# Pinned TensorE order in the second layer, one block transpose placed later, the second product one tile further behind

## The chip, the cores and the metric

The kernel runs on one core of a Trainium2 chip. The metric is device time in microseconds of one execution; the time before is the median of three runs. The engines are TensorE (PE, its weight loads shown apart as PEld), VectorE (DVE), ScalarE (ACT), GpSimd (POOL) and SyncE (SP), which issues nearly all DMAs here.

## What is computed

Three stages follow each other: attention within chunks of 64 tokens, a first feed-forward layer with g = h·cos(h), and a second feed-forward layer whose activation is h·softmax(h), normalised over its 1024 columns. All is in float32. The change touches the second layer alone.

```python
def _moe2_ref(x, w_in, w_out, g_ln):          # x 4608x512, w_in 512x1024, w_out 1024x512
    h = x @ w_in
    h_max = np.max(h, axis=-1, keepdims=True)
    e = np.exp(h - h_max)
    sm = e / (np.sum(e, axis=-1, keepdims=True) + 1e-09)
    solu = h * sm
    mu = np.mean(solu, axis=-1, keepdims=True)
    var = np.mean((solu - mu) ** 2, axis=-1, keepdims=True)
    ln = (solu - mu) / np.sqrt(var + 1e-06) * g_ln
    return (ln @ w_out).astype(np.float32)
```

## The kernel before

**Precision.** Every float32 operand of a product is split into a high and a low part, and a product is three matmuls: high·high, high·low, low·high, each 128x128 weights against 512 columns.

**The second layer, first product.** The 4608 tokens are 36 tiles of 128, taken two at a time: 18 pairs, i = 0 to 17. The product x·w_in of a pair is made from seven block products (a Strassen-like scheme), spread over four segments: `pair(i, seg)` issues 12, 12, 6 and 12 matmuls for seg 0, 1, 2, 3, that is 42 for a pair, on the lines L862 to L864 in `prod`. The results land in PSUM tiles h2 that rotate over three buffers, so a segment takes over the buffer of the segment three before it: (i, 3) that of (i, 0). ACT (L902) and DVE (L887, L890) add the blocks up in SBUF; L902 and the first L890 free the buffer of (i, 0). Of the four SBUF tiles that the pairs' results rotate over, the one of the second tile of an odd pair is taken from the pool tag "w".

**Between the products.** `stats(i, e)` and `norm(i, e)` (e = 0, 1 for the two tiles of the pair) make softmax and normalisation one pair later, on ACT, DVE and POOL. `blocks32(i, e)` transposes the result in 32x32 blocks on DVE into a tile bt that holds four tiles, group j (L964). When the four tiles of group j are there, after pair 2j+1, `shuffle(j)` issues 16 DMAs on SP (L974) that carry the blocks to four tiles lt, which are the transposed tiles t = 4j to 4j+3. `split_ln(t)` makes the high and low parts lh (ACT) and ll (DVE), both on L104.

**Second product.** `mm_o(t, half)` issues 12 matmuls of ln·w_out (L992, L993, L994: lh·whi, lh·wlo, ll·whi), half 0 for the first 512 of the 1024 rows, half 1 for the others; `store(t)` copies the sum (ACT, L998, tile os) and issues four DMAs on SP. Tiles lt, lh, ll and the odd pairs' result share the pool tag "w" of 32 slots with the weights of the layer (22 of them).

**The order.** Segments are counted x = 4i + seg. The last loop goes over x: it traces the segment (i, seg), then at even x the split of the next tile and the store of the one before, and then 12 matmuls of tile t = 2i − 7 + seg//2. So in the source's order TensorE alternates 12 (or 6) matmuls of h with 12 of o, and the first tile of group j, t = 4j, comes at the place (2j+3, 2), three segments after its shuffle was traced at (2j+2, 3). Segments up to (3, 0) are traced in the loop of the first layer, beside its last steps.

**Who orders.** The framework plans the order of each engine's instructions itself, by its own account of when operands and buffers are there, and by the source's order among those that are ready. An instruction issued through an `InOrder` wrapper while its flag is set is pinned behind all that was traced before it on its engine. In the second layer no instruction is pinned before the change. Each engine then works through its own list in that order.

Of the kernel before, what the change touches and what calls it, by code (L numbers as in the profile page):

```python
# [29 lines left out]
def kernel(  # L30
# [12 lines left out]
    nc = tc.nc  # L43
# [8 lines left out]
    SUB = T // P  # L52
    NI = NT // P
    KD = DM // P
    NF = F1 // P
    NF2 = F2 // P
# [52 lines left out]
            return call  # L109

    pe, act, dve = InOrder(nc.tensor), InOrder(nc.scalar), InOrder(nc.vector)
    sync = InOrder(nc.sync, in_order_loads)

    def split(src, hi, lo, mul=None):

        if mul is None:
            act.activation(out=hi, in_=src, func=AF.Copy)
            dve.tensor_tensor(out=lo, in0=src, in1=hi.bitcast(F32), op=ALU.subtract)
        else:
            nc.scalar.activation(out=hi, in_=src, func=AF.Copy, scale=mul)  # L120
            nc.vector.scalar_tensor_tensor(
                out=lo, in0=src, scalar=mul, in1=hi.bitcast(F32), op0=ALU.mult, op1=ALU.subtract
            )
# [32 lines left out]
    def wtile(dt, name, n=1024):  # L156
        return wp.tile([P, n], dt, tag="w", name=name)
# [528 lines left out]
    def load_y(i):  # L686
        t = sp_.tile([P, 7 * 256], F32, tag="st", name="yr")
        nc.sync.dma_start(out=t, in_=y_dram[i // 2][i % 2])
        yr[i] = t
# [19 lines left out]
    if True:  # L709
# [23 lines left out]
        for c in range(4):  # L733
            sync.dma_start(
                out=gcol[32 * c:32 * (c + 1)],
# [103 lines left out]
        for i in range(SUB, NU):  # L839
            j, o = divmod(UNITS[i][0] * CH, T)  # L840
# [17 lines left out]
        def prod(i, ps, operand, key):  # L858
            for kk in range(2):
                a, b = (y[i][operand][:, kk * P:(kk + 1) * P] for y in (yh, yl))  # L860
                whi, wlo = w2in[key, kk]
                nc.tensor.matmul(out=ps, lhsT=a, rhs=whi, start=kk == 0, stop=False)  # L862
                nc.tensor.matmul(out=ps, lhsT=a, rhs=wlo, start=False, stop=False)  # L863
                nc.tensor.matmul(out=ps, lhsT=b, rhs=whi, start=False, stop=kk == 1)  # L864

        def h2tile(i, e):
            x = (2 * i + e) % 4
# [51 lines left out]
        def stats(i, e):  # L919
            h2 = hA.pop((i, e))  # L920
            nm = ap_.tile([P, 1], F32, tag="nm", name="nm", bufs=4)
            ss = ap_.tile([P, 1], F32, tag="ss", name="ss", bufs=4)
            nc.vector.tensor_scalar(out=nm, in0=tops.pop((i, e, 1)), scalar1=-1.0, scalar2=None, op0=ALU.mult)
            ex = ap_.tile([P, 1024], F32, tag="t", name="e", bufs=2)
            nc.scalar.activation(out=ex, in_=h2, func=AF.Exp, bias=nm, accum_out=ss)
            nc.vector.tensor_scalar(out=ss, in0=ss, scalar1=1e-9, scalar2=None, op0=ALU.add)
            nc.vector.reciprocal(out=ss, in_=ss)
            mu = ap_.tile([P, 1], F32, tag="mu", name="mu", bufs=4)
            nc.vector.scalar_tensor_tensor(
                out=h2, in0=h2, scalar=ss, in1=ex, op0=ALU.mult, op1=ALU.mult, accum_out=mu  # L930
            )
            nc.vector.tensor_scalar(out=mu, in0=mu, scalar1=-1.0 / F2, scalar2=None, op0=ALU.mult)
            va = ap_.tile([P, 1], F32, tag="va", name="va", bufs=4)
            nc.scalar.activation(out=ex, in_=h2, func=AF.Square, bias=mu, accum_out=va)
            nc.vector.tensor_scalar(
                out=va, in0=va, scalar1=1.0 / F2, scalar2=1e-6, op0=ALU.mult, op1=ALU.add
            )
            rs = ap_.tile([P, 1], F32, tag="rs", name="rs", bufs=4)
            nc.gpsimd.tensor_tensor(out=rs, in0=va, in1=nhalf, op=ALU.pow)
            nc.gpsimd.tensor_tensor(out=mu, in0=mu, in1=rs, op=ALU.mult)  # L940
            solu[i, e], nmu[i, e], rstd[i, e] = h2, mu, rs

        def norm(i, e):
            so = solu[i, e]
            nc.scalar.activation(
                out=so, in_=so, func=AF.Identity, scale=rstd.pop((i, e)), bias=nmu.pop((i, e))
            )
# [6 lines left out]
        def blocks32(i, e):  # L954
            j, n = i // 2, i % 2 + 2 * e
            if j not in blks:
                if j == 0:
                    blks[j] = [wtile(F32, "bt").rearrange("p (q n t) -> p q n t", q=8, n=SUB) for _ in range(4)]
                else:
                    t = sp[0].tile([P, 32, SUB, 32], F32, tag="bt", name="bt", bufs=1)  # L960
                    blks[j] = [t[:, 8 * c:8 * (c + 1)] for c in range(4)] + [t]
            src = solu.pop((i, e)).rearrange("p (b f) -> p b f", f=32)
            if j:
                nc.vector.transpose(out=blks[j][4][:, :, n], in_=src)  # L964
            else:
                for c in range(4):
                    nc.vector.transpose(out=blks[j][c][:, :, n], in_=src[:, 8 * c:8 * (c + 1)])

        def shuffle(j):
            b = blks.pop(j)  # L970
            for a in range(4):
                l = wtile(F32, "lt")
                for c in range(4):
                    nc.sync.dma_start(  # L974
                        out=l[32 * c:32 * (c + 1)],
                        in_=b[c][32 * a:32 * (a + 1)].rearrange("p q n t -> p (q n t)"),
                    )
                lnp[j, a] = l

        def split_ln(j, a):  # L980
            hi, lo = wtile(F32R, "lh"), wtile(F32R, "ll")
            split(lnp.pop((j, a)), hi[:], lo[:])
            lnh[j, a], lnl[j, a] = (x.rearrange("p (f c) -> p f c", c=P) for x in (hi, lo))

        def mm_o(j, a, half):
            if half == 0:
                ops[j, a] = ps_h.tile([P, DM], F32, tag="h", name="o")
            o = ops[j, a]
            for f in range(half * NF2 // 2, (half + 1) * NF2 // 2):
                hi, lo = lnh[j, a][:, f], lnl[j, a][:, f]  # L990
                whi, wlo = w2out[f]
                nc.tensor.matmul(out=o, lhsT=hi, rhs=whi, start=(f == 0), stop=False)  # L992
                nc.tensor.matmul(out=o, lhsT=hi, rhs=wlo, start=False, stop=False)  # L993
                nc.tensor.matmul(out=o, lhsT=lo, rhs=whi, start=False, stop=(f == NF2 - 1))  # L994

        def store(j, a):
            s = sp[0].tile([P, DM], F32, tag="os", name="os")
            nc.scalar.activation(out=s, in_=ops.pop((j, a)), func=AF.Copy)  # L998
            for n in range(SUB):
                t0 = j * T + n * P + 32 * a  # L1000
                queue = nc.scalar if n % 2 and (j, a) == (NJ - 1, SUB - 1) else nc.sync
                queue.dma_start(out=out[t0:t0 + 32, :], in_=s[32 * n:32 * (n + 1)])

        def segment(i, seg):

            if i < NPAIR:
                pair(i, seg)
            if 0 <= i - 1 < NPAIR:
                e = seg // 2
                if seg % 2 == 0:  # L1010
                    stats(i - 1, e)
                else:
                    norm(i - 1, e)
                    blocks32(i - 1, e)
                    if e and (i - 1) % 2:
                        shuffle((i - 1) // 2)
            if i + 1 < NPAIR:
                if seg == 1:
                    load_y(i + 1)
                elif seg == 3:  # L1020
                    split_y(i + 1)
# [4 lines left out]
        for n in range(NSTEP + LAG + 1):  # L1026
# [50 lines left out]
            if rest >= 6:  # L1077
                segment((rest - 6) // 4, (rest - 6) % 4)
# [1 line left out]
        sp.append(ctx.enter_context(tc.tile_pool(name="sp", bufs=2, reuse_waits="tile")))  # L1080


        LAG2 = 7
        first_seg = 4 * EARLY + 1
        split_ln(0, 0)
        for x in range(first_seg, 2 * (NI + LAG2) + 4):
            i, seg = divmod(x, 4)
            segment(i, seg)
            t, half = 2 * i - LAG2 + seg // 2, seg % 2
            if half == 0:  # L1090
                if 0 <= t + 1 < NI:
                    split_ln(*divmod(t + 1, SUB))
                if 0 <= t - 1 < NI:
                    store(*divmod(t - 1, SUB))
            if 0 <= t < NI:
                mm_o(*divmod(t, SUB), half)


# [25 lines left out]
```

## Time and profile before

| what | us |
|---|---|
| median of three runs | 1317.0 (1316.44 to 1317.3) |
| the profiled execution | 1315.48 |
| its span, first to last instruction | 1313.7 |
| TensorE busy | 1270.9, 97% of the span |
| VectorE busy | 977.1, 74% |
| ScalarE busy | 789.3, 60% |

The span begins with attention, then runs the first layer to about 948 us and the second layer from 867 us on, the two overlapping; from 964 us on only the second layer is left. The granted clock of TensorE was 0.992 in the mean. A matmul's row shows its start and a duration of 0.39 us; since matmuls are pipelined, the step from one start to the next is what counts.

### The profile page before, as it was taken

How to read it: one execution, taken by the hardware profiler on the slowest of the kernel's cores; microseconds unless marked ns; L12 is line 12 of the kernel's file. 1: busy time of each engine (PE TensorE's matmuls, PEld its weight loads, DVE VectorE, ACT ScalarE, POOL GpSimd, SP SyncE). 2: the span in 40 equal slices, each digit the busy share in tenths (PEclk: the TensorE clock that was granted, in tenths of full speed). 3: DMA queues.
4: the chain of work that ended last, by engine and by line, in shares of the span. 5: the costliest groups of instructions: out<-in, count | busy, mean ns of one | idle time of the engine just before them, and what ended most of it. 6: DMA issues, size and time to landing. Idle time of an engine off the chain costs nothing.

```text
span 1313.7 us, 20245 instructions
## 1 busy us (share of the span) xinstructions
PE 1270.9 (97%) x7652; PEld 1016.4 (77%) x7652; DVE 977.1 (74%) x1608; ACT 789.3 (60%) x1143; POOL 30.7 (2%) x79
## 2 busy tenths in 40 slices
PE   5899999999999999999999999999989999999998
PEld 4566777888887787888887888888768888888886
DVE  4887988676779879878878866667786686766751
ACT  4877876666655656556556545537665655655552
POOL 0000000000000000000000000000110000000000
PEclk9899999999999999999999999999989999999999
DMA  9942344331344344353343410450464543445224
GB/s 243 212 108 82 111 132 92 90 77 30 58 135 135 63 133 133 65 124 97 78 108 97 95 27 1 150 215 28 154 190 114 149 131 99 122 111 145 64 63 107
DMA packets 240930, 143.44 MB, mean 109 GB/s; under 512 B 176832, under 2 KB 217280, under 8 KB 239296
## 3 DMA queue, kind: packets, MB, share of 16 engines
q1 hardware_dynamic: 240736, 142.02, 41.4%
q8 instruction: 60, 0.98, 0.3%
q14 instruction: 38, 0.31, 0.1%
q10 hardware_dynamic: 96, 0.13, 0.0%
HBM read 83.63 MB, written 39.58 MB: 94 GB/s over the span
## 4 chain that ended last, share of the span: by engine, by line
PE 76%; DVE 10%; ACT 5%; issue 4%; SPq 3%; DMA 2%; POOL 0%; ACTq 0%; DVEq 0%; POOLq 0%
PE h L570 8%; PE y L637 8%; PE y L638 7%; PE y L639 7%; PE h L572 7%; PE h L571 7%; PE o L994 5%; PE o L992 5%; PE o L993 5%; PE h L862 4%; PE h L864 3%; PE h L863 3%; SPq L104 3%; DVE z L104 2%; PE x L104 1%
## 5 line engine op out<-in xcount | busy, mean ns | idle before, releaser
L570 PE MATMUL h<-xh,whi 128*128 128x512 f32 x576 | 232.6, 404 | 1.6 <-ACT xh L104 1.3
L571 PE MATMUL h<-xl,whi 128*128 128x512 f32 x576 | 226.2, 393 | 0.9 <-DVE xl L104 0.9
L572 PE MATMUL h<-xh,wlo 128*128 128x512 f32 x576 | 226.2, 393 | 0.1
L637 PE MATMUL y<-gh,whi 128*128 128x512 f32 x544 | 213.0, 397 | 4.8 <-ACT gh L104 3.8
L638 PE MATMUL y<-gl,whi 128*128 128x512 f32 x544 | 215.3, 396 | 0.3 <-DVE gl L104 0.3
L639 PE MATMUL y<-gh,wlo 128*128 128x512 f32 x544 | 214.9, 395 | 0.0
L599 ACT ACTIVATE r<-r 128x512 f32<-128x512 f32 x144 | 90.8, 631 | 166.0 <-DVE r L593 165.7
L607 DVE SCALAR_TENSOR_TENSOR hs<-r,hs 128x512 f32<-128x512 f32 x136 | 93.7, 689 | 81.6 <-ACT r L600 81.2
L570 PEld LDWEIGHTS h<-xh,whi 128*128 128x128 f32 x576 | 108.8, 189 | 27.9 <-issue 1.6
L104 ACT ACTIVATE gh<-hs 128x512 fp32r<-128x512 f32 x136 | 85.5, 629 | 74.0 <-DVE hs L607 71.0
L571 PEld LDWEIGHTS h<-xl,whi 128*128 128x128 f32 x576 | 108.7, 189 | 25.0 <-issue 1.7
L572 PEld LDWEIGHTS h<-xh,wlo 128*128 128x128 f32 x576 | 108.6, 189 | 24.2 <-issue 0.5
L104 DVE TENSOR_TENSOR gl<-hs,gh 128x512 fp32r<-128x512 f32 x136 | 93.4, 687 | 44.8 <-ACT gh L104 44.6
L637 PEld LDWEIGHTS y<-gh,whi 128*128 128x128 f32 x544 | 101.4, 188 | 31.7 <-ACT gh L104 7.5
L638 PEld LDWEIGHTS y<-gl,whi 128*128 128x128 f32 x544 | 102.2, 188 | 26.2 <-DVE gl L104 2.3
L639 PEld LDWEIGHTS y<-gh,wlo 128*128 128x128 f32 x544 | 102.1, 188 | 23.6
L577 ACT ACTIVATE hs<-h 128x512 f32<-128x512 f32 x144 | 85.2, 592 | 56.7 <-PE h L572 46.2
L992 PE MATMUL o<-whi,lh 128*128 128x512 f32 x288 | 113.5, 394 | 1.6 <-ACT lh L104 1.6
L994 PE MATMUL o<-whi,ll 128*128 128x512 f32 x288 | 113.2, 393 | 0.7 <-DVE ll L104 0.5
L993 PE MATMUL o<-wlo,lh 128*128 128x512 f32 x288 | 113.3, 393 | 0.0
L590 DVE SCALAR_TENSOR_TENSOR r<-kt,hs 128x512 f32<-128x512 int32 x144 | 99.1, 688 | 16.4 <-ACT kt L585 13.9
L862 PE MATMUL h<-whi,yh 128*128 128x512 f32 x252 | 99.6, 395 | 9.9 <-DVE tp L890 9.9
(112 smaller groups left out, 2078.3 us busy)
## 6 DMA issues: line engine op xcount, KB each, us to landing
lt<-bt SPq DMA_DIRECT2D x144, 128.0 KB
yr<-yd SPq DMA_DIRECT2D x18, 896.0 KB
yd<-ts SPq DMA_DIRECT2D x18, 512.0 KB
out<-os SPq DMA_DIRECT2D x142, 64.0 KB
vi<-in_v SPq DMA_DIRECT2D x64, 128.0 KB
qi<-in_q SPq DMA_DIRECT2D x224, 32.0 KB
ki<-in_k SPq DMA_DIRECT2D x224, 32.0 KB
st<-in_moe_w_in SPq DMA_DIRECT2D x10, 512.0 KB
```

Source lines behind the costliest of these rows:

```text
L104: ins = getattr(self.engine, name)(*args, **kwargs)
L570: nc.tensor.matmul(out=t, lhsT=wa, rhs=xh[j][:, kk, :], start=(kk == 0), stop=False)
L571: nc.tensor.matmul(out=t, lhsT=wa, rhs=xl[j][:, kk, :], start=False, stop=False)
L572: nc.tensor.matmul(out=t, lhsT=wb, rhs=xh[j][:, kk, :], start=False, stop=(kk == KD - 1))
L590: nc.vector.scalar_tensor_tensor(out=r, in0=kt, scalar=-TWO_PI_HI, in1=h, op0=ALU.mult, op1=ALU.add)
L637: nc.tensor.matmul(out=o, lhsT=wa, rhs=a, start=head, stop=False)
L638: nc.tensor.matmul(out=o, lhsT=wa, rhs=b, start=False, stop=False)
L639: nc.tensor.matmul(out=o, lhsT=wb, rhs=a, start=False, stop=last)
L862: nc.tensor.matmul(out=ps, lhsT=a, rhs=whi, start=kk == 0, stop=False)
L992: nc.tensor.matmul(out=o, lhsT=hi, rhs=whi, start=(f == 0), stop=False)
L993: nc.tensor.matmul(out=o, lhsT=hi, rhs=wlo, start=False, stop=False)
L994: nc.tensor.matmul(out=o, lhsT=lo, rhs=whi, start=False, stop=(f == NF2 - 1))
```

## The change

There are four edits.

1. A second wrapper `pe2` of TensorE with a flag of its own, `late`, off at first. The matmuls of `prod` and of `mm_o` go through it. The flag is set just before the last loop, so from the segment (3, 1) on each matmul of both products is pinned behind everything that was traced before it on TensorE.
2. In `segment`, the block transposes of the pair's first tile, `blocks32(i−1, 0)`, are traced in seg 2, ahead of the statistics of the second tile, and no longer in seg 1. Those of the second tile stay in seg 3.
3. The tile of the second product is read from a list `order` with one entry for each half pair: seven empty places, tiles 0 to 13, one empty place, tiles 14 to 35, one empty place. So tiles 0 to 13 stand where they stood, the segments (10, 2) and (10, 3) have no matmul of the second product, and from tile 14 on each tile comes one half pair (two segments) later than before.
4. Split and store follow the list: the split of the next entry and the store of the entry before.

The number of instructions and their shapes are the same.

```diff
--- before.py
+++ after.py
@@ -109,6 +109,9 @@
             return call
 
     pe, act, dve = InOrder(nc.tensor), InOrder(nc.scalar), InOrder(nc.vector)
+
+    late = [False]
+    pe2 = InOrder(nc.tensor, late)
     sync = InOrder(nc.sync, in_order_loads)
 
     def split(src, hi, lo, mul=None):
@@ -859,9 +862,9 @@
             for kk in range(2):
                 a, b = (y[i][operand][:, kk * P:(kk + 1) * P] for y in (yh, yl))
                 whi, wlo = w2in[key, kk]
-                nc.tensor.matmul(out=ps, lhsT=a, rhs=whi, start=kk == 0, stop=False)
-                nc.tensor.matmul(out=ps, lhsT=a, rhs=wlo, start=False, stop=False)
-                nc.tensor.matmul(out=ps, lhsT=b, rhs=whi, start=False, stop=kk == 1)
+                pe2.matmul(out=ps, lhsT=a, rhs=whi, start=kk == 0, stop=False)
+                pe2.matmul(out=ps, lhsT=a, rhs=wlo, start=False, stop=False)
+                pe2.matmul(out=ps, lhsT=b, rhs=whi, start=False, stop=kk == 1)
 
         def h2tile(i, e):
             x = (2 * i + e) % 4
@@ -989,9 +992,9 @@
             for f in range(half * NF2 // 2, (half + 1) * NF2 // 2):
                 hi, lo = lnh[j, a][:, f], lnl[j, a][:, f]
                 whi, wlo = w2out[f]
-                nc.tensor.matmul(out=o, lhsT=hi, rhs=whi, start=(f == 0), stop=False)
-                nc.tensor.matmul(out=o, lhsT=hi, rhs=wlo, start=False, stop=False)
-                nc.tensor.matmul(out=o, lhsT=lo, rhs=whi, start=False, stop=(f == NF2 - 1))
+                pe2.matmul(out=o, lhsT=hi, rhs=whi, start=(f == 0), stop=False)
+                pe2.matmul(out=o, lhsT=hi, rhs=wlo, start=False, stop=False)
+                pe2.matmul(out=o, lhsT=lo, rhs=whi, start=False, stop=(f == NF2 - 1))
 
         def store(j, a):
             s = sp[0].tile([P, DM], F32, tag="os", name="os")
@@ -1006,13 +1009,17 @@
             if i < NPAIR:
                 pair(i, seg)
             if 0 <= i - 1 < NPAIR:
-                e = seg // 2
+
+
+                if seg == 2:
+                    blocks32(i - 1, 0)
                 if seg % 2 == 0:
-                    stats(i - 1, e)
+                    stats(i - 1, seg // 2)
                 else:
-                    norm(i - 1, e)
-                    blocks32(i - 1, e)
-                    if e and (i - 1) % 2:
+                    norm(i - 1, seg // 2)
+                if seg == 3:
+                    blocks32(i - 1, 1)
+                    if (i - 1) % 2:
                         shuffle((i - 1) // 2)
             if i + 1 < NPAIR:
                 if seg == 1:
@@ -1080,19 +1087,21 @@
         sp.append(ctx.enter_context(tc.tile_pool(name="sp", bufs=2, reuse_waits="tile")))
 
 
-        LAG2 = 7
+
         first_seg = 4 * EARLY + 1
+        order = [None] * 7 + list(range(14)) + [None] + list(range(14, NI)) + [None]
         split_ln(0, 0)
-        for x in range(first_seg, 2 * (NI + LAG2) + 4):
-            i, seg = divmod(x, 4)
-            segment(i, seg)
-            t, half = 2 * i - LAG2 + seg // 2, seg % 2
+        late[0] = True
+        for x in range(first_seg, 2 * len(order)):
+            segment(*divmod(x, 4))
+            t, half = order[x // 2], x % 2
             if half == 0:
-                if 0 <= t + 1 < NI:
-                    split_ln(*divmod(t + 1, SUB))
-                if 0 <= t - 1 < NI:
-                    store(*divmod(t - 1, SUB))
-            if 0 <= t < NI:
+                nxt, prev = order[min(x // 2 + 1, len(order) - 1)], order[x // 2 - 1]
+                if nxt is not None:
+                    split_ln(*divmod(nxt, SUB))
+                if prev is not None:
+                    store(*divmod(prev, SUB))
+            if t is not None:
                 mm_o(*divmod(t, SUB), half)
 
 
```

## Rows read from the trace of the kernel before

**Rows 1.** The page, first part: busy time, share of the span, instructions

```profile
PE 1270.9 (97%) x7652; PEld 1016.4 (77%) x7652; DVE 977.1 (74%) x1608; ACT 789.3 (60%) x1143; POOL 30.7 (2%) x79
```

**Rows 2.** Busy time by stretch: length, PE, PEld, DVE, ACT, POOL, granted clock, DMA

```profile
957.90:970.90 13.00, 6.84 (x20) 4.67 (x19) 9.77 (x17) 8.45 (x11) 1.47 (x4) 0.74 0.91 269
970.90:1007.80 36.90, 36.90 (x164) 30.23 (x162) 23.12 (x53) 22.54 (x32) 3.66 (x8) 1.00 0.48 129
...
1009.20:1283.40 274.20, 270.88 (x1188) 222.25 (x1186) 189.47 (x401) 159.59 (x218) 19.19 (x52) 1.00 0.41 108
1283.40:1290.10 6.70, 4.54 (x13) 3.25 (x13) 3.04 (x3) 3.65 (x4) 0.00 (x0) 0.75 0.91 207
```

**Rows 3.** Waits of TensorE from 900 us on: total, times, longest

```profile
PE h L862 <- DVE tp L890: 9.9, 8, 6.0
```

**Rows 4.** Timeline of TensorE about 1050 us: start, duration, line

```profile
1049.42 0.39 PE L864 MATMUL h<-whi,yl 128*128 128x512 f32 x1
1050.36 0.50 PE L862 MATMUL h<-whi,yh 128*128 128x512 f32 x1 [0.55 <-DVE tp L890]
1050.70 0.40 PE L992 MATMUL o<-whi,lh 128*128 128x512 f32 x1
...
1052.53 0.39 PE L994 MATMUL o<-whi,ll 128*128 128x512 f32 x1
```

**Rows 5.** Timeline of ScalarE at the same place

```profile
1048.49 0.60 ACT L998 ACTIVATE os<-o 128x512 f32<-128x512 f32 x1 [2.83 <-PE o L994]
1048.98 0.59 ACT L902 ACTIVATE h<-h 128x512 f32<-128x512 f32 x1
1049.46 2.96 ACT L104 ACTIVATE lh<-lt 128x1024 fp32r<-128x1024 f32 x3
```

**Rows 6.** Timeline of VectorE at the same place

```profile
1049.61 0.69 DVE L890 CUSTOM_DVE_ANT_0 h<-h,h 128x512 f32<-128x512 f32 x1 [6.13 <-ACT h L902]
...
1051.02 1.22 DVE L104 TENSOR_TENSOR ll<-lt,lh 128x1024 fp32r<-128x1024 f32 x1
```

**Rows 7.** Timeline of TensorE where the first layer has ended

```profile
964.32 0.79 PE L862 MATMUL h<-whi,yh 128*128 128x512 f32 x1 [6.02 <-DVE tp L890]
964.90 0.63 PE L992 MATMUL o<-whi,lh 128*128 128x512 f32 x1
...
967.81 0.80 PE L994 MATMUL o<-whi,ll 128*128 128x512 f32 x1
...
969.24 0.39 PE L994 MATMUL o<-whi,ll 128*128 128x512 f32 x1
...
978.40 0.50 PE L864 MATMUL h<-whi,yl 128*128 128x512 f32 x1
```

**Rows 8.** Timeline of ScalarE at that place

```profile
962.77 1.04 ACT L104 ACTIVATE lh<-lt 128x1024 fp32r<-128x1024 f32 x1
```

**Rows 9.** Timeline of VectorE at that place

```profile
966.53 1.22 DVE L104 TENSOR_TENSOR ll<-lt,lh 128x1024 fp32r<-128x1024 f32 x1
```

**Rows 10.** Timeline of TensorE at the last group's first tile

```profile
1283.06 0.39 PE L994 MATMUL o<-whi,ll 128*128 128x512 f32 x1
1285.08 0.50 PE L992 MATMUL o<-whi,lh 128*128 128x512 f32 x1 [1.63 <-ACT lh L104]
...
1286.34 0.55 PE L994 MATMUL o<-whi,ll 128*128 128x512 f32 x1 [0.53 <-DVE ll L104]
1286.68 0.63 PE L992 MATMUL o<-whi,lh 128*128 128x512 f32 x1
...
1290.09 0.39 PE L994 MATMUL o<-whi,ll 128*128 128x512 f32 x1
```

**Rows 11.** Timeline of ScalarE at that place

```profile
1283.48 0.60 ACT L998 ACTIVATE os<-o 128x512 f32<-128x512 f32 x1 [4.84 <-PE o L994]
1283.98 1.05 ACT L104 ACTIVATE lh<-lt 128x1024 fp32r<-128x1024 f32 x1
```

**Rows 12.** Timeline of SyncE's queue at that place

```profile
1279.10 10.06 SPq L974 DMA_DIRECT2D lt<-bt  x16
```

## The prediction

> **What bounds the kernel now.** I read the page first, then the waits of TensorE, its granted clock by stretches, and the order on each engine at the places where TensorE stands. TensorE is busy 97% of the span [rows 1], and the change takes no matmul away, so only the time in which TensorE waits or runs at the lower clock can be won. The waits name nearly one reason: eight waits of the first product for DVE L890, 9.9 us in all, the longest 6.0 [rows 3], so the other seven are 3.9/7 = 0.55 us each. The busy times by stretch show where the loss lies [rows 2]. From 957.9 to 970.9 us TensorE is busy for 6.84 of 13.00 us at a mean clock of 0.74. From 970.9 to 1007.8 it is busy throughout. From 1009.2 to 1283.4 it is idle for 274.2 − 270.9 = 3.3 us, six of the seven short waits (the seventh stands just before). From 1283.4 to 1290.1 it is busy for 4.54 of 6.70 us at 0.75. In the full stretch [rows 2] 164 matmuls, 163 steps, fill 36.9 us, so neighbours start 0.227 us apart at full clock. The 13.0 us at the start hold 18 steps of that length, 4.1 us, so 8.9 are lost there; the 7.0 us around the end (from 1283.06 to 1290.09 [rows 10]) hold 12 steps, 2.7 us, so 4.3 are lost; a short wait costs 0.83 (below). About 19 us is all that the second layer could give back.
>
> **How a short wait comes about.** They come every two pairs, at the end of the segment (2j+3, 2) for j = 1 to 7; I show the one at 1050 us. ScalarE copies the sum of the previous tile (os, L998), which must wait for that tile's last matmul, then does L902 of (2j+3, 0), whose product had ended two segments before, and then three lh in a row [rows 5]. L902 is in the list behind os and has to wait with it. VectorE does L890 behind L902, then, after one more addition, the first ll [rows 6]. TensorE has nothing it may start before L890 frees the PSUM buffer: h starts at 1050.36, 0.94 us after the matmul before; then two o with the new lh, five h, and the first o with ll only at 1052.53, when ll is long done [rows 4, 6]. The planner thus has put h of (2j+3, 3) in front of o of tile 4j: the h cover the time in which ll is made. That ScalarE's place of L902 comes from the shared pool tag "w" (the shuffle's lt, the result that L902 writes and the new lh and ll draw their slots from it in this order of the source) is what I conclude from the source; the row order os, L902, lh is what the trace shows.
>
> **The pinned matmuls (edit 1).** The source has o of the tile first at this place, then h of (2j+3, 3). ScalarE and VectorE are not pinned, and what sets their order there isn't touched, so I keep it. Then TensorE goes: last h at 1049.42; first o when lh is there, 1049.46 + 1.05 = 1050.51 (one lh takes 1.05 us [rows 11]), start at 1050.56, as a matmul starts 0.05 us after the lh that it waits for [rows 10, 11]; the third o needs ll, 1051.02 + 1.22 = 1052.24 [rows 6], start at 1052.29; the fourth 0.34 us later (the step behind a wait [rows 10]), 1052.63. Without waiting that fourth would start at 1049.42 + 4·0.227 = 1050.33. The loss is 2.30 us. Before: after h at 1050.36 the next matmul starts at 1050.70 [rows 4], against 1049.42 + 2·0.227 = 1049.87, a loss of 0.83. The edit costs 1.47 us at each place, 7·1.47 = **10.3 us**. Bounds: −5.8 us (7·0.83, if the 12 o, 2.7 us of work, find their lh ready and cover L890) and +21 us (each wait also brings on the lower clock, as at the end: a mean of 0.75 over 6.70 us is 3.35 us at 1.2 instead of 2.4 GHz, which costs 1.7 us [rows 2]).
>
> It is the nature of TensorE's queue that decides here. At 964.32 h starts after its wait and the first o at 964.90 [rows 7], though its lh was ready at 962.77 + 1.04 = 963.81 [rows 8]: a matmul behind a waiting one didn't pass it. The Trainium skill says the same (TensorE: Matmul & The Clock Gate, Part 2, Step-by-step): matmuls stay in program order, only weight loads are pulled ahead. The trace agrees; could a matmul pass, edit 1 would cost 0 instead of 10.3 us and the sum would end near 1319.
>
> **The start.** The place (3, 2) has the same shape with a longer wait, 6.0 us [rows 3, 7]. Now h runs from 964.32, with two o between, and the o that needs ll (966.53 + 1.22 = 967.75 [rows 9]) comes at 967.81. Pinned, TensorE starts with o at 963.86, does two and stands until 967.80. By then it has done 2 matmuls instead of 7. Five matmuls at full clock are 1.1 us. The full step came back at 969.24, after five us of matmuls [rows 7]; with the standing it may come back later, and 3.35 us more at the lower clock, as at the end [rows 2], is another 1.7. And h of (4, 0) had to wait for its yl until 978.40, though one and a half tiles of o were drawn in front of it [rows 7]; in the source's order only half a tile stands in between, and yl is made behind statistics that now come later: 0 to 2.5 us. Taken: **+2.5 us**, ends +1.1 and +5.3.
>
> **The later block transposes (edit 2).** Nothing is added. They run on VectorE, 74% busy [rows 1] and idle for 6.13 us ahead of the place in question [rows 6]; a later place in the source lowers their rank among ready instructions only. Their successors, the shuffle's 16 DMAs on SP, wait for the second tile's transposes anyway, which don't move. At (3, 2) both run before L890, in TensorE's wait. I take **0**, ends −1 and +1 (one transpose more or less ahead of an L890 at one of the places).
>
> **Eight tiles behind (edits 3 and 4).** In pairs 11 to 17 the tile at (2j+3, 2) becomes 4j−1 instead of 4j. Its lt landed long before, but its split is traced at the same place as that of 4j was, behind the shuffle and behind the result of the odd pair. So I expect lh behind os and L902 as now and the same 2.30 us. The empty half pair lets h of (10, 2), (10, 3) and (11, 0) follow each other; their buffers were freed a pair before, so 0 (up to +1). The splits and stores that follow the list issue the same four DMAs each, one half pair later on SP, whose queue nobody waits for until the end: 0.
>
> **The end.** With eight tiles left behind the last h, o of tile 32 comes 24 matmuls, 5.4 us, later after it. The first lt of the last group is issued at 1279.10 [rows 12]. But the trace shows lh of tile 32 directly behind os of tile 31, whose copy waits for TensorE itself, with no wait for a DMA between [rows 11]. As long as ScalarE keeps that order, TensorE stands after tile 31 for os, lh and then ll as now, 1.63 + 0.53 us [rows 10], and the clock falls likewise. Taken **0**; ends −4.3 (lh goes ahead of os) and +1.
>
> **The sum** on the profiled execution: 1315.5 + 10.3 + 2.5 = 1328.3. That execution is 1.5 us under the median, so 1329.8 in the median's terms: 1330.
>
> **Rivals.**
> 1. *Faster: the planner sets L902 or the new lh ahead of os.* With TensorE's order fixed, the other engines are planned anew; if L902 comes ahead of os at all places, L890 is done before (2j+3, 2) ends, the seven waits vanish (−5.8), and at the end lh ahead of os gives −4.3; the start stays at +2.5: 1317 − 7.6 = 1309. It turns the sign from four free places on, with the end won as well. For it: ScalarE is idle for 2.83 us before os [rows 5], so there is room. Against it: the order at these places comes from the slots, and all eight show the same.
> 2. *Mixed.* Only the places from pair 11 on are free, since tile 4j−1 is ready earlier: 3·1.47 − 4·0.83 + 2.5 = +3.6, or with the end won −0.7: 1316 to 1321.
> 3. *Longer stands bring the lower clock.* Stands of 1.63 and 0.53 us with 0.36 us of work between did so at the end [rows 2, 10]; those of 0.75 and 1.0 us that I expect may do so at most of the places: +10 on the forecast, 1336 to 1345.
> 4. *It does nothing.* The planner's order is the source's nearly everywhere, and at the places it exchanges work of equal length: 1317.
>
> **How the numbers follow.** The measurement tells 0.2% (2.6 us) from no change. Chances: forecast 0.53 (1322 to 1336), rival 1 0.20 (1304 to 1313), rival 2 0.13 (half of it within 0.2%), rival 3 0.09, rival 4 0.05. Slower: 0.53 + 0.09 + 0.05 of rival 2 = 0.67; same 0.05 + 0.06 = 0.11; faster 0.20 + 0.02 = 0.22. For 8 in 10 the range runs from 1309 (half of rival 1 below it) to 1338.
>
> **What would show it.** Right: at the odd pairs from 5 on TensorE shows two waits, the first o for ACT lh and the third for DVE ll, 0.7 to 1.1 us each, and no wait of h for L890; about 1.5 us more idle per two pairs between 1010 and 1280. Wrong for edit 1: ScalarE's list shows L902 or lh ahead of os, and no waits there. Wrong for the end: no idle TensorE at tile 32. Wrong for the start: less than 9 us lost between 958 and 982.

## The result and the profile after

| | before | after |
|---|---|---|
| median | 1317.0 us (5 runs, 1314.2 to 1317.3) | 1335.7 us (5 runs, 1335.1 to 1336.8) |
| ratio | | 1.0147, 95% interval 1.0132 to 1.0162 |
| span of the profiled run | 1313.7 us | 1333.9 us |
| TensorE busy | 1270.9 us | 1279.5 us |
| mean granted clock | 0.992 | 0.984 |

The change makes the kernel 1.5% slower. The waits of TensorE from 900 us on (in all, times, longest) have changed their names; compare [rows 3]:

```profile
PE o L104 <- ACT lh L104: 12.5, 9, 5.6
PE o L104 <- DVE ll L104: 10.1, 9, 2.7
```

No h waits for L893 (L890 of before) any more. Each time it is an o that waits, first for lh and then for ll: once at the start, at seven places, and once at the end. The start, compare [rows 7]:

```profile
964.79 0.79 PE L104 MATMUL o<-whi,lh 128*128 128x512 f32 x1 [5.58 <-ACT lh L104]
...
968.72 0.80 PE L104 MATMUL o<-whi,ll 128*128 128x512 f32 x1 [2.72 <-DVE ll L104]
...
973.94 0.40 PE L104 MATMUL h<-whi,yl 128*128 128x512 f32 x1
```

The pinned matmuls all show L104, the wrapper's line; the other lines moved by three.

The place shown in [rows 4 to 6] now stands at 1056 us. TensorE (start, duration, line; in brackets idle time and its releaser), ScalarE, VectorE:

```profile
1056.09 0.39 PE L104 MATMUL h<-whi,yl 128*128 128x512 f32 x1
1057.23 0.50 PE L104 MATMUL o<-whi,lh 128*128 128x512 f32 x1 [0.76 <-ACT lh L104]
1057.57 0.40 PE L104 MATMUL o<-wlo,lh 128*128 128x512 f32 x1
1058.95 0.62 PE L104 MATMUL o<-whi,ll 128*128 128x512 f32 x1 [0.99 <-DVE ll L104]
1059.37 0.63 PE L104 MATMUL o<-whi,lh 128*128 128x512 f32 x1
...
1062.36 0.51 PE L104 MATMUL o<-wlo,lh 128*128 128x512 f32 x1
1062.70 0.39 PE L104 MATMUL o<-whi,ll 128*128 128x512 f32 x1
```

```profile
1055.15 0.60 ACT L1001 ACTIVATE os<-o 128x512 f32<-128x512 f32 x1 [2.83 <-PE o L104]
1055.65 0.59 ACT L905 ACTIVATE h<-h 128x512 f32<-128x512 f32 x1
1056.12 2.95 ACT L104 ACTIVATE lh<-lt 128x1024 fp32r<-128x1024 f32 x3
```

```profile
1056.27 0.69 DVE L893 CUSTOM_DVE_ANT_0 h<-h,h 128x512 f32<-128x512 f32 x1 [6.13 <-ACT h L905]
...
1057.68 1.22 DVE L104 TENSOR_TENSOR ll<-lt,lh 128x1024 fp32r<-128x1024 f32 x1
```

ScalarE's and VectorE's lists at this place are those of before. TensorE's is not: the h that covered lh and ll come behind the twelve o. It stands for 0.76 and 0.99 us. From 1059.37 to 1062.36 its steps are 0.43 us, nearly twice as long, and the clock granted there is 0.50, the lower of its two levels (1.2 GHz):

```profile
1059.40:1062.30 2.90, 2.90 (x8) 2.31 (x7) 2.90 (x6) 1.06 (x1) 0.00 (x0) 0.50 0.00 0
```

That doesn't happen at every place. The busy time by stretch (length, PE, PEld, DVE, ACT, POOL, granted clock, DMA share, GB/s), the same eight microseconds at five of the seven places:

```profile
1056.00:1064.00 8.00, 6.25 (x20) 4.39 (x19) 7.62 (x11) 4.13 (x5) 0.00 (x0) 0.79 0.13 33
1100.80:1108.80 8.00, 6.25 (x26) 4.54 (x25) 7.70 (x11) 3.02 (x5) 0.00 (x0) 1.00 0.13 33
1138.50:1146.50 8.00, 6.25 (x27) 4.56 (x26) 7.71 (x11) 4.18 (x6) 0.00 (x0) 1.00 0.49 149
1181.50:1189.50 8.00, 6.25 (x20) 4.36 (x19) 7.60 (x11) 4.18 (x5) 0.00 (x0) 0.79 0.13 33
...
1271.00:1279.00 8.00, 6.25 (x20) 4.36 (x19) 7.64 (x11) 4.00 (x5) 0.00 (x0) 0.79 0.13 34
```

PE is busy for 6.25 us in all of them, but does 26 or 27 matmuls at clock 1.00 and 20 at 0.79. Busy time doesn't show the loss; the count and the clock do.

For all comparisons below I use one measure: from a trace's matmul starts, each gap between neighbours less the full step of 0.227 us, summed by place (gaps that exceed the step by less than 0.02 us are left out; counted from 943 us on; 0.74 us near 944 are in every kernel and stand only in the last column).

| kernel | start (957 to 985) | the seven places | end (tile 31 or 32) | in all |
|---|---|---|---|---|
| before | 8.8 | 7 x 0.83 = 5.8 | 4.3 | 19.8 |
| after | 11.7 | 5 x 3.90, 2 x 2.30 = 24.1 | 2.7 | 39.2 |

The difference is 19.4 us; the span grew by 20.2, of which 0.9 us are already there at the last matmul before the start (958.82 against 957.91), ahead of the pin.

### The profile page after: what moved, and what is told of

Same layout as the page of the kernel before. It is cut to its first block, busy times and chain, and to the rows that moved or that the text cites. A ratio compares the mean times of both kernels' runs of the same rounds, so it can differ in the third digit from the quotient of the medians.

```text
span 1333.9 us, 20243 instructions
## 1 busy us (share of the span) xinstructions
PE 1279.5 (96%) x7652; PEld 1020.1 (76%) x7652; DVE 979.3 (73%) x1608; ACT 789.7 (59%) x1143; POOL 30.3 (2%) x79
## 4 chain that ended last, share of the span: by engine, by line
PE 70%; DVE 11%; issue 8%; ACT 6%; SPq 3%; DMA 2%; POOL 1%; ACTq 0%; DVEq 0%; POOLq 0%
PE o L104 12%; PE h L104 8%; PE h L573 7%; PE y L640 7%; PE y L641 7%; PE y L642 7%; PE h L575 7%; PE h L574 7%; SPq L104 2%; DVE z L104 2%; PE x L104 1%; PE sc L104 1%; PE y L633 1%; PE pt L104 1%; SPq L977 1%
## 5 line engine op out<-in xcount | busy, mean ns | idle before, releaser
L104 ACT ACTIVATE gh<-hs 128x512 fp32r<-128x512 f32 x136 | 85.5, 629 | 74.0 <-DVE hs L610 71.1
L104 PE MATMUL o<-whi,lh 128*128 128x512 f32 x288 | 117.0, 406 | 12.5 <-ACT lh L104 12.5
L104 PE MATMUL o<-whi,ll 128*128 128x512 f32 x288 | 117.2, 407 | 10.1 <-DVE ll L104 10.1
L104 DVE TENSOR_TENSOR gl<-hs,gh 128x512 fp32r<-128x512 f32 x136 | 93.4, 687 | 44.8 <-ACT gh L104 44.6
L104 PE MATMUL o<-wlo,lh 128*128 128x512 f32 x288 | 116.2, 403 | 0.0
L596 DVE SCALAR_TENSOR_TENSOR r<-kt,r 128x512 f32<-128x512 int32 x144 | 99.2, 689 | 2.8
```

The costliest lines, as they stand in the source:

```text
L104: ins = getattr(self.engine, name)(*args, **kwargs)
L596: nc.vector.scalar_tensor_tensor(out=r, in0=kt, scalar=-TWO_PI_LO, in1=r, op0=ALU.mult, op1=ALU.add)
```

## The experiments

**Theory.** The pin (edit 1) carries the whole loss; edits 2 to 4 cost nothing. It costs because ScalarE and VectorE keep lists that were made for another order of TensorE: os, L902, lh, with ll behind. **Rivals:** the lag of eight tiles or the block transposes carry part of it; or a pinned TensorE costs by itself, because no matmul can go ahead while another waits.

### 1. The pin alone

```diff
+    late = [False]
+    pe2 = InOrder(nc.tensor, late)
...
         split_ln(0, 0)
+        late[0] = True
```

The six matmuls of `prod` and `mm_o` go through `pe2`, as in the change.

> The kernel before with TensorE's matmuls of the second layer pinned and nothing else changed (edit 1 alone). Theory A (the pin carries the whole loss): 1332 to 1337 us; at the seven places o stands for ACT lh about 0.76 us and for DVE ll about 1.0 us, 1.47 us more lost at each than before, and the clock falls at about five of them for about 1.6 us each; the start loses about 3 us more than before. Rival B (lag 8 brings the falls of the clock, since three of the five lie in the part with lag 8): 1328 to 1331, falls at pairs 5 and 7 only. Rival C (the block transposes carry a part): below 1328.

Measured: 1336.4 us (1329.9 to 1338.1), ratio 1.0139 (1.0113 to 1.0166), as slow as the whole change. Lost: start 12.1, places 4 x 3.9 and 3 x 2.30 = 22.5, end 2.7, in all 38.0. The same stands of 0.76 and 0.99 us stand at all seven places, yet the clock fell at the first three and the last, where the changed kernel held it at the third and fourth only:

```profile
1101.70:1109.70 8.00, 6.26 (x20) 4.37 (x19) 7.72 (x11) 4.03 (x5) 0.00 (x0) 0.79 0.13 33
1189.50:1197.50 8.00, 6.25 (x26) 4.54 (x25) 7.69 (x11) 4.08 (x6) 0.00 (x0) 1.00 0.13 35
```

The falls are not tied to lag 8 (rival B): this kernel has them at 1102 and 1276 us with a lag of seven throughout, and the changed kernel has none at 1101 us, with a lag of seven there, and three with eight. They differ from run to run of one kernel, too: its runs took 1329.9 us at a mean clock of 0.989 up to 1338.1 at 0.983, 8.2 us apart, as much as five falls of 1.6 us would cost.

### 2. Everything but the pin

The changed kernel without the pin:

```diff
-        late[0] = True
```

> The changed kernel without the pin: later block transposes and the lag of eight tiles from pair 11 on (edits 2 to 4). Theory A: 1316 to 1318 us, the seven places as before (h waits for L893, about 0.83 us lost each), and the end about 0 to 2 us cheaper. Rival B (lag 8 carries part of the loss): 1320 to 1326. Rival C (the block transposes do): 1319 or more with the loss between 958 and 975 us.

Measured: 1316.4 us, ratio 1.0000 (0.9990 to 1.0009). The waits are those of [rows 3]:

```profile
PE h L104 <- DVE tp L893: 9.9, 8, 6.0
PE o L104 <- ACT lh L104: 1.6, 1, 1.6
PE o L104 <- DVE ll L104: 1.2, 2, 0.7
```

Six places lose 0.83 us as before; the one where the list has its gap (1127 us) loses 1.8, since o waits there for ll as well, 0.72 us; the end loses 2.7, without a fall of the clock. In sum edits 2 to 4 cost nothing that can be measured.

### 3. Pinned, with h first at the odd pairs

From the changed kernel:

```diff
-            if t is not None:
+            at = x // 4 % 2 and x // 4 < NPAIR
+            if t is not None and not (at and x % 4 == 2):
+                if at and x % 4 == 3:
+                    mm_o(*divmod(t, SUB), 0)
                 mm_o(*divmod(t, SUB), half)
```

> The changed kernel, all pinned as it is, but at each odd pair the source puts the first half of the tile of segment 2 behind the h of segment 3: TensorE has 12 h, 2.7 us of work, ahead of the o that needs the new lh and ll. Theory A (what costs is the order at eight places, not the pin): the seven places fall back to about 0.83 us, no o waits there, no fall of the clock, the start back to about 9 us: 1314 to 1319 us. Rival B (the pin costs in other places or the lag does): 1325 to 1336. Rival C (12 h in a row run into their own waits for VectorE's additions): stands of 1 to 2 us at h and 1322 to 1332.

Measured: 1318.8 us, ratio 1.0021 (1.0012 to 1.0031). TensorE is pinned as in the changed kernel, and nearly the whole loss is gone:

```profile
PE h L104 <- DVE tp L893: 9.9, 8, 6.0
PE h L104 <- DVE yl L104: 2.8, 1, 2.8
```

Seven places lose 0.82 or 0.83 us, and the clock falls at none. What remains is the start, 13.4 us: with the order moved there too, h of (4, 0) waits 2.8 us for its yl. So it is not the pin as such but which work stands in front of the wait.

### 4. Pinned, ScalarE's lh and os pinned as well, an own buffer for the odd pair's result

From the changed kernel:

```diff
+    act2 = InOrder(nc.scalar, late)
-            split(lnp.pop((j, a)), hi[:], lo[:])
+            src = lnp.pop((j, a))
+            act2.activation(out=hi, in_=src, func=AF.Copy)
+            nc.vector.tensor_tensor(out=lo, in0=src, in1=hi.bitcast(F32), op=ALU.subtract)
...
```

The copy os goes through `act2`, too, and the result that L902 of (2j+3, 0) writes gets a buffer of its own in the pool `sp`.

> The changed kernel, with a buffer of its own for the second result of the odd pairs instead of a slot of the shared pool, and ScalarE's lh and os pinned as well, which puts each lh ahead of the os that the source has behind it. Theory A (the stands come from ScalarE's order os, L905, lh): no stands at the places, none at tile 32, the start still as in the changed kernel: 1317 - 5.8 - 4.3 + 3 = about 1310 us (1307 to 1314). Rival B (lh of a new group waits for its DMAs and now holds os back, and with it the PSUM buffer of the next o): stands of 1 to 3 us at the places, 1320 to 1340.

Measured: 1338.9 us, ratio 1.0168 (1.0153 to 1.0183), against my theory, and not by the rival's mechanism either. ScalarE does as it should: lh at 1051.26 and 1052.68, the first of them done three us ahead of the o that needs it at 1055.35. But VectorE, left to the planner, has ll behind the additions of segment 2, which wait for TensorE (L893 and L896 are L887 and L890 of before, and ll shows L990). VectorE, then the third o:

```profile
1051.47 1.42 DVE L893 TENSOR_TENSOR h<-h,h 128x512 f32<-128x512 f32 x2 [2.29 <-PE h L104]
1055.55 0.69 DVE L896 CUSTOM_DVE_ANT_0 h<-h,h 128x512 f32<-128x512 f32 x1 [2.66 <-PE h L104]
...
1056.77 2.35 DVE L990 TENSOR_TENSOR ll<-lt,lh 128x1024 fp32r<-128x1024 f32 x2
```

```profile
1058.03 0.79 PE L104 MATMUL o<-whi,ll 128*128 128x512 f32 x1 [2.07 <-DVE ll L990]
```

The third o stands for 2.1 us, at six of the seven places. TensorE and ScalarE in a common order were not enough; VectorE's list decided.

### 5 to 8. The shuffle drawn apart

```diff
-        shuffle((i - 1) // 2)
+        shuffle((i - 1) // 2, range(1))
...
+                    shuffle(x // 8 - 1, range(1, 4))
```

The second argument says which lt are issued; the last line stands at x = 8j + 12, behind the split and the store. Experiment 5 has this in the kernel before, the first shuffle left whole; 6 adds the pin of experiment 1; 7 draws the first shuffle apart, too; 8 is 7 in the kernel of experiment 2. Where the expectations of 7 and 8 name a first kernel or the one before, these are 5 and 7. What 7 and 8 add:

```diff
                     load_y(i + 1)
+                    if i == EARLY:
+                        shuffle(0, range(1, 4))
```

> The kernel before, TensorE unpinned, but of each shuffle from the second on only the first lt is traced where all four were; the other three follow behind the split of the next tile, one segment later. Theory A (the slots of the shared pool, drawn in the source's order lt, lt, lt, lt, L902's result, lh, ll, are what holds L902 and lh behind os): ScalarE does lh and L902 ahead of os, the seven waits of 0.83 us lost each go away, the start and the end stay: 1317 - 5.8 = 1311 us (1309.5 to 1313.5). Rival B (the order os, L902, lh has another reason, such as the times that the planner gives them): no change, 1315 to 1318. Rival C (the later lt come too late for tiles 4j+1 to 4j+3): stands for lh or DMA at those tiles, 1319 or more.

> Edit 1 alone (the pin), together with the shuffle drawn apart: one lt, the split of the next tile, then three lt. Theory A (the pin costs only where ScalarE's order lets the new lh and ll come late): no stand at the seven places, no fall of the clock there, the start as with the pin alone (+3), the end as before: 1317 - 5.8 + 3 = 1314 us (1312 to 1316). Rival B (the pin costs by itself, since TensorE can no longer fill a wait): over 1322 us, with stands of 0.7 to 2 us at some tiles.

> As the first kernel of this call, and the first shuffle is drawn apart too: its three later lt follow behind the load of y of the fourth pair. Theory A: L902 of (3, 0) and lh of tile 0 no longer wait behind the four lt; o of tile 0 (24 matmuls, 5.4 us) fills part of the 8.9 us lost between 958 and 971: 1302 to 1309 us. Rival B (the start is bound by the chain from the statistics of pair 2, whatever the order): the same as the first kernel of this call within 1.5 us. Rival C (a later lt or yl is late and TensorE stands there): 1312 or more.

> As the kernel before this one, with the changed kernel's order list (eight tiles behind from pair 11 on) and its later block transposes, TensorE unpinned. Theory A (eight tiles are worth only what they save at the end: 2.7 us lost there in the two runs that have it, against 4.3): 0 to 2 us under the kernel before this one. Rival B (with eight tiles the pool's ten free slots are short and lh comes late again): stands at the places from pair 11 on, 2 to 6 us more.

Measured, in this order: 1330.8 us (ratio 1.0108, 1.0092 to 1.0123), 1331.6 (1.0112, 1.0095 to 1.0129), 1345.0 (1.0217, 1.0198 to 1.0236), 1336.5 (1.0156, 1.0140 to 1.0171). All are slower than before, in new places. In the first, the places at 1007, 1049 and 1091 us lose nothing: L902 and lh stand ahead of os there, at 1049 us like this:

```profile
1040.66 0.58 ACT L902 ACTIVATE h<-h 128x512 f32<-128x512 f32 x1
1041.13 1.05 ACT L104 ACTIVATE lh<-lt 128x1024 fp32r<-128x1024 f32 x1
...
1047.61 0.60 ACT L998 ACTIVATE os<-o 128x512 f32<-128x512 f32 x1 [0.81 <-PE o L994]
```

That is what theory A expects, but it doesn't show that the slots are the reason: the edit also traces twelve DMAs later, and experiments 9, 11 and 12 have L902 and lh ahead of os with the pool and the shuffle as before. The slots alone don't force that order. From 1138 us on, lh of the following tiles stands behind an e that waits for the maxima of the pair just finished; ScalarE there:

```profile
1137.75 1.15 ACT L925 ACTIVATE e<-h,nm 128x1024 f32<-128x1024 f32 x1 [6.92 <-DVE nm L923]
...
1138.90 1.04 ACT L104 ACTIVATE lh<-lt 128x1024 fp32r<-128x1024 f32 x1
```

That costs 2.9 us at each of three places and, with falls of the clock, 15.6 from 1269 us on. The second loses nothing at the first two places, 0.17 us at the third, and 15.9 at 1142, where h waits for a yh that ScalarE's list has behind a pair's statistics:

```profile
PE h L104 <- ACT yh L104: 11.5, 1, 11.5
```

The third tells of the start. The stretch in which the kernel before loses 8.9 us holds no stand at all, compare [rows 2]:

```profile
957.00:971.00 14.00, 14.00 (x63) 11.60 (x62) 11.84 (x28) 9.50 (x14) 2.13 (x4) 1.00 0.93 228
```

The 8.9 us lost at the start are a matter of order, too; but from 985 us on this kernel loses 46.7 us, with o waiting for lh eleven times, 24.1 us, and with falls of the clock. The fourth (lag 8) doesn't separate the list's gap from the new waits. The lesson of the four: moving one step changes the planner's lists of all engines, for better at one place and for worse at another, and the sum was worse each time.

### 9 to 12. Which engines are pinned

From the kernel before: VectorE's L887, L890 and ll through a third wrapper, ScalarE's lh and os as in experiment 4, the pool as before; in 10 only the matmuls, in 11 only the two other engines. The order of the source: lh and os alternate, each lh a tile ahead of the o that reads it.

```diff
+    dve2 = InOrder(nc.vector, late)
...
+            late[0] = 20 <= x < 70
```

The last line is that of 9 to 11; in 12 the flag is set behind `split_ln(0, 0)`, as in the change. The first kernel that the expectations of 10 and 11 name is that of 9.

> The kernel before, with the pin on three engines instead of one, from (5, 0) up to (17, 1): TensorE's matmuls, ScalarE's lh and os, VectorE's L890, L887 and ll, all in the source's order; start and end are left to the planner as before. Theory A (a pinned TensorE costs only because ScalarE and VectorE are left in an order made for another one; with all three in the source's order, which has lh and ll a tile ahead, there is nothing to wait for): no stands at the seven places, start as before (8.9 us lost), end 2 to 4 us lost: 1307 to 1312 us. Rival B (ScalarE pinned to lh ahead of os waits for the lt of a new group, as in the run with lh and os pinned alone): stands of 1 to 2 us at the places, 1316 to 1335.

> As the first kernel of this call, with TensorE alone pinned in the same stretch. Theory A: the two stands, 1.47 us more lost than before at each of the places of pairs 5 to 15 (six of them, or seven), start and end as before: 1316.5 + 9 to 10 = 1326 us without the lower clock, and up to 1335 with a fall of it (1.6 us) at each. Rival B (the pin costs through the start, which shifts the rest): 1316 to 1320.

> As the first kernel of this call, with ScalarE and VectorE pinned in the same stretch and TensorE left to the planner. Theory A (what matters is that lh and ll come a tile ahead, whoever fills the wait): the places free but for one or two, 1307 to 1314 us. Rival B (all three have to be pinned together): stands of 1 to 3 us at most places, 1318 or more.

> Edit 1 as the change has it, from the second layer's first o on, with ScalarE's lh and os and VectorE's L890, L887 and ll pinned as well. Theory A: against the pin alone (1336) the stands at the places go or become under 0.8 us each, the start keeps its 2 to 3 us more, no or few falls of the clock: 1308 to 1318 us. Rival B (the pin on TensorE costs by itself): over 1325.

| pinned | median | ratio to before | start | places | end | in all |
|---|---|---|---|---|---|---|
| TensorE, ScalarE, VectorE, (5, 0) to (17, 1) | 1311.6 | 0.9968 (0.9956 to 0.9980) | 9.0 | 0 | 4.1 | 14.0 |
| TensorE alone, same stretch | 1330.7 | 1.0114 (1.0101 to 1.0128) | 9.2 | 4 x 3.9, 2 x 2.30, 0.83 | 2.7 | 33.8 |
| ScalarE and VectorE, same stretch | 1310.3 | 0.9956 (0.9943 to 0.9970) | 9.0 | 0 | 4.1 | 13.9 |
| all three from the first o on | 1309.1 | 0.9950 (0.9937 to 0.9964) | 9.7 | 0 | 2.3 | 12.7 |

Same matmuls, same pin of TensorE: 1336.4 us with the two other engines left alone (experiment 1), 1309.1 with them in the same order. That is 25 us by the ratios to before and 27 by the medians, for the lists of two engines that are idle for a quarter and more of the time. With ScalarE and VectorE ordered, pinning TensorE makes no difference that these runs could tell (1311.6 and 1310.3). The waits of TensorE that are left in the kernel with ScalarE and VectorE pinned, compare [rows 3]:

```profile
PE h L866 <- DVE tp L104: 6.0, 1, 6.0
PE o L998 <- ACT lh L104: 1.7, 1, 1.7
PE o L1000 <- DVE ll L104: 0.5, 1, 0.5
```

The seven short ones are gone. The middle of the second layer in the last kernel, by stretch, and the place of [rows 4 to 6] in it, ScalarE and then VectorE:

```profile
1000.00:1268.00 268.00, 268.00 (x1184) 221.93 (x1183) 190.34 (x407) 158.59 (x220) 27.37 (x52) 1.00 0.44 115
```

```profile
1048.05 0.58 ACT L906 ACTIVATE h<-h 128x512 f32<-128x512 f32 x1
1048.52 1.05 ACT L104 ACTIVATE lh<-lt 128x1024 fp32r<-128x1024 f32 x1
1049.47 0.58 ACT L104 ACTIVATE os<-o 128x512 f32<-128x512 f32 x1
```

```profile
1048.66 0.69 DVE L104 CUSTOM_DVE_ANT_0 h<-h,h 128x512 f32<-128x512 f32 x1 [2.69 <-ACT h L906]
...
1049.60 1.23 DVE L104 TENSOR_TENSOR ll<-lt,lh 128x1024 fp32r<-128x1024 f32 x1 [0.25 <-ACT lh L104]
```

L902 (L906 here) and lh stand ahead of os, ll is done at 1050.83, and the first o with ll starts at 1051.45, without a wait. These three kernels beat both the one before and the changed one.

## Why the prediction was right, and which term was too small

The direction and the mechanism held; the time came out 5.7 us above the forecast and inside the range.

- **The places (+10.3).** Right to the hundredth: the two stands at every odd pair from 5 on, a loss of 2.30 us where the clock stayed, 1.47 more than 0.83, seven times. (The upper bound given there, +21, comes to 22.2 from its own terms, 10.3 and 7 x 1.7; nothing rests on it.) Experiment 1 shows that edit 1 alone does it, experiment 10 that it needs nothing from the start.
- **The start (+2.5).** It rose by 2.9 us in the changed kernel, 3.3 with the pin alone. As forecast, o waits for lh (5.58 us) and for ll (2.72), and the full step comes back later, at 973.94 instead of 969.24. The wait for yl that I allowed for did not come there; experiment 3 has it, 2.8 us.
- **Edits 2 to 4 (0).** Right: ratio 1.0000 without the pin. There the place behind the list's gap costs 1.0 us more, the bound that I had given, and the end loses 1.6 less, so the zero is also a sum of two small terms.
- **The end (0).** The stands were as forecast, 1.63 and 0.53 us, but the clock didn't fall behind them: 2.7 us lost instead of 4.3. That is 1.6 us that I had not forecast; compare [rows 10]:

```profile
1301.50 0.50 PE L104 MATMUL o<-whi,lh 128*128 128x512 f32 x1 [1.63 <-ACT lh L104]
...
1302.76 0.50 PE L104 MATMUL o<-whi,ll 128*128 128x512 f32 x1 [0.53 <-DVE ll L104]
1303.09 0.39 PE L104 MATMUL o<-whi,lh 128*128 128x512 f32 x1
```

- **The clock (rival 3): the term that was mis-sized.** The forecast had no fall at the seven places, and gave 0.09 to a rival with +10 us for falls at most of them. The falls came at five of seven, at the price that the rival had, 1.6 us each, 8.0 in all. 1330 and 8.0, less the 1.6 of the end, is 1336.4, against 1335.7 measured. I had one example of a fall behind short stands, longer by 0.4 us in sum than mine, and priced it well; to give it a chance of one in eleven had no row behind it. (Between its two stands lay two matmuls, 0.73 us from 1285.08 on, and not the 0.36 that rival 3 says.)
- **What was luck.** Five of seven is "most of the places", so what happened is the forecast's order with rival 3's clock on top. The time lies 0.3 us inside the forecast's band (1322 to 1336); one more fall, 1.6 us, at either of the two other places or at the end would have put it into rival 3's.
- **Rival 1** (L902 or lh ahead of os, 1309) didn't happen, since TensorE's pin left ScalarE's list alone. Experiments 9, 11 and 12 bring that order about by pins on ScalarE and VectorE: 1309.1 to 1311.6 us. That is near the 1309 of the rival, but not by its terms: the places gave the 5.8 us, while the start cost 0.2 to 0.9 us instead of 2.5 and the end gave 0.2 to 2.0 instead of 4.3. What I held against the rival, that the slots fix the order, doesn't hold by itself, as these three show.
- **Program order on TensorE.** The h behind the o, whose buffer L893 had freed by 1056.96, start at 1062.93, after all twelve o; nothing passed the third o while it stood. The Trainium skill (TensorE: Matmul & The Clock Gate, Part 2, Step-by-step) has matmuls stay in program order, and the trace agrees.

**Open.** What decides whether one and the same stand is followed by the lower clock (below). Whether one of ScalarE and VectorE, or fewer of VectorE's three operations, would have been enough; no run pins them apart. Whether the start of experiment 7 and the middle of experiment 12 go together; it wasn't tried. Which of the three faster kernels is the fastest.

## What to carry to other kernels

Pinning one engine to the source's order, while the planner keeps its own for the engines that feed it, can turn covered waits into open ones: read, at each place where the order changes, what now stands in front of the first instruction that waits, and what stands in the list of the engine that it waits for. If an order is to be written out, write it for all engines that take part in it; here that made 25 to 27 us of difference with the same matmuls. And price each new stand of TensorE twice, without and with the lower clock behind it, when the trace shows even one such case.

## What the runs showed of the hardware

Two stands of 0.76 and 0.99 us with two matmuls between them were followed by the lower clock in 13 of 20 cases (5 of 7 in the changed kernel, 4 of 7 with the pin alone, 4 of 6 in experiment 10), with the same instructions around them. It costs 1.6 us each (3.9 lost against 2.30): the step is 0.43 instead of 0.227 us for some three us, at a granted clock of 0.50. Longer stands were no surer sign: single ones of 2.07 us in experiment 4 were followed by it in 4 of 6 cases, and pairs that add up to 2.33 us in experiment 5 (1.09 and 1.24, twice; 1.63 and 0.70) in none of three. Single stands of about 0.55 us were never followed by it, in 21 cases (before, experiments 2, 3 and 10). The stands of 1.63 and 0.53 us at the end were followed by it in the kernel before and in experiments 9 and 11, and not in the changed kernel and in experiments 1, 2, 3 and 10. So the fall is no function of the stand alone, and runs of one kernel differ by it: 8.2 us in experiment 1. The Trainium skill (TensorE: Matmul & The Clock Gate, Part 1: The HAM clock gate, What's actually happening) states that the number of slow matmuls at a kernel's start varies between runs of one kernel; no run here shows that, but the like is seen behind stands in the kernel's middle.
